# Keep-warm products, another order behind attention, and five instead of four of eight chunks turned by DMA, in a fused attention and mixture-of-experts kernel

## The chip, the core and the metric

The kernel runs on one core of a Trainium2 chip. The metric is the device time of one execution in microseconds (us), median of several runs. The core's engines are TensorE (PE; its weight loads are shown apart as PEld), VectorE (DVE), ScalarE (ACT) and GpSimd (POOL); SyncE (SP) issues all the kernel's DMAs. Each engine works through its own list of instructions in order, and they wait for one another through semaphores.

## The reference

Three stages follow one another, all in fp32.

```python
# 1. gated linear attention: 4 batches, 8 heads, 768 steps, head size 40; state C (40x40), n, m per head
m_new = max(f + m, i); f_s = exp(f + m - m_new); i_s = exp(i - m_new)
C = f_s * C + i_s * outer(v, k);  n = f_s * n + i_s * k
y = sigmoid(o_gate) * (C @ q) / max(abs(n . q), 1)          # x: 3072 tokens x 320
# 2. soft mixture: 8 experts x 4 slots
logits = x @ phi                                             # 3072 x 32
d = softmax(logits over tokens);  slot_input = d.T @ x       # 32 x 320
slot_out = relu(slot_input @ w1[e]) @ w2[e]                  # 320 -> 1024 -> 320 for each expert
x = softmax(logits over slots) @ slot_out
# 3. dense block
h = x @ w_in                                                 # 3072 x 1024
u = h * softmax(h);  ln = (u - mean(u)) / sqrt(var(u) + 1e-6) * g_ln
out = ln @ w_out                                             # 3072 x 320
```

## The kernel before, in words

**Attention.** The tokens are cut into 24 units of 128 tokens (6 chunks of the sequence times 4 batches). A unit's work is cut into some forty steps, and strings of step names (`FIRST`, `ORDER`, `LAST`, lines 33 to 50) give the order in which all engines' instructions are written, unit by unit; no scheduler changes it. In the last two units (`LAST`) the step `qm` (L524) multiplies the queries of unit 23 by decay factors on GpSimd, `x` (L360) forms a unit's gated output on GpSimd, `sl` (L439) adds a group of four units into the slot sums, and `mean` (L509) averages the output weights with the product of a constant and `wsum`, a sum of weight blocks that GpSimd forms (L741). A unit's output lies in one of five buffers `x_t`, used in turn. Next to all this the weights are loaded and decoded. Early on, `warm_up(6)` (L538) runs products whose result nobody reads.

**Behind attention.** Lines 747 to 949 are a chain for the last unit and the experts: its output is normalised, transposed (L763) and multiplied by `phi` for all four units of the group together (L772, `lt_last`), the maximum is taken (L775), weights of the softmax are formed, slot inputs summed and transposed (L804, `siT`), then come the experts' first and second products (L836, L893), the slots' outputs times `w_in` (L934, `swc_ps`) split into a high and a low fp32r part (`swh`, `swl`) and spread into two tiles `swf` (L947, L948). `w_low` (L927) makes the low part of the output weights on VectorE.

**The dense block.** 24 tiles of 128 tokens are pipelined. `FIN_START` (L56) orders the filling of the pipeline, `FIN` (L57) each later tile; a token such as `e:3` writes step `e` for the tile three ahead. The steps:

- `h` (L962): two products on TensorE give 1024 values a token; `m` (L967) their maximum, on VectorE; `e` (L974) exp, on ScalarE; `u` (L981) their product, on VectorE.
- `T0` (L1008): TensorE transposes four of the eight 128-column chunks of u into PSUM. The other four go through DMA: `d` (L1014) copies them on GpSimd into two planes of 16-bit halves (`up`), `t` (L1019) lets a DMA transpose these into `tp`, and `g` (L1024) joins the halves on GpSimd into `uf`. Tiles 0 and 1 use TensorE for all eight.
- `x0`, `x1` (L1031 on ScalarE, L1029 on GpSimd): the high fp32r part `uh` of each half; `y0`, `y1` (L1035, VectorE): the low part `ul`.
- `k0` to `k7`, `a`, `b` (L1043, L1044, L1046): three products for each chunk; `a` is the two with `uh`, `b` the one with `ul`.
- `q`, `s`, `v`: variance and scale; `o` (L1050): scaled output on ScalarE, and its DMA.

Of the kernel before, what the change touches and what calls it, by code (L numbers as in the profile page):

```python
# [7 lines left out]
F32 = mybir.dt.float32  # L8
# [4 lines left out]
U16 = mybir.dt.uint16  # L13
# [6 lines left out]
T = TOK = 128  # L20
# [19 lines left out]
 "numa xT tm1 scA numb scB den0 xTc tm2 nt ntc sig0 R o0 den2 o1 exp sg sig1 kw o3 wA wB o2 sl qm x sig2",  # L40
 "one o0 o1 o2 o3 xT numa numb xTc den0 den2 sg mean x",
# [14 lines left out]
FIN_START = "c:1 h:0 cc:1 m:0 c:2 h:1 c:3 cc:2 m:1 e0:0 e1:0 u0:0 c:4 e0:1 T0:0 x0:0 cc:3 u1:0 u0:1 T1:0 y0:0 cc:4 h:2 x1:0 m:2 c:5 y1:0 e1:1 v:0 T0:1 u1:1 e:2 x0:1 u:2 k0:0 a6:0 q:0 a4:0 d:2 a5:0 cc:5 b4:0 b6:0 s:0 y0:1 a7:0 k3:0 b5:0 k1:0 h:3 k2:0 m:3 b7:0 T1:1 T0:2 x1:1 v:1 y1:1 k0:1 e:3 a7:1 t:2 v:2 x0:2 u:3 a6:1 o:0 q:2 k3:1 h:4 k2:1 b4:1 b5:1 y0:2 a5:1 b6:1 g:2 k1:1 a4:1 d:3 m:4 q:1 h:5 e:4 k0:2 m:5 t:3 x1:2 b7:1 g:3 T0:3 k1:2 x0:3 a4:2 y1:2 k3:2 a5:2 a7:2 u:4 b4:2 d:4 s:1 o:1 a6:2 e:5 k2:2 y0:3 b6:2 s:2 v:3 b5:2 t:4 x1:3 b7:2"  # L56
# [7 lines left out]
def tile_kernel(  # L64
# [441 lines left out]
    def wo_mean(fs):  # L506
        wm = GT["warm"][:, 1].rearrange("p r t -> p (r t)")[:, 0:DM]
        for f in fs:
            PE.matmul(wm, on128, wo[:, 5 + f, :] if f else wsum, start=f == 0, stop=f == 2)  # L509
        return wm  # L510
# [84 lines left out]
    pe_gate(0)  # L595
    gate_nat(0)
# [24 lines left out]
    def ops(i):  # L621
# [31 lines left out]
        else:  # L653
            T["one"] = po_last
            T["mean"] = lambda: wo_mean(range(2))
        if i == NU - 2:
            T["R"], T["exp"], T["qm"] = pe_qscale, st_qscale, st_qmul
# [57 lines left out]
    for i in range(NU):  # L715
# [33 lines left out]
    ph0 = ps_sc.tile([128, 512], F32, tag="s1", name="ph0")  # L749
    A.activation(out=ph0, in_=ones[:, 0:1].to_broadcast([128, 512]), func=AF.Copy, scale=0.0)  # L750
    pe_xT(L - 1)
    st_xT(L - 1)
    U[L]["sg"] = kvo_t[L % 4][:, 2 * DM + NH:].rearrange("p (h d) -> p h d", h=NH)
# [13 lines left out]
    lg = bank("misc", "lt_last")  # L767
    PE.matmul(lg[:, 128:129], ident, lt_t[:, T:T + 1], start=True, stop=True)
    for k in range(3):
        kk = min(128, DM - 128 * k)  # L770
        for j in range(NB):
            PE.matmul(lg[32 * j:32 * j + 32, 0:128], phi_sb[0:kk, k, :], U[4 * g + j]["xT"][0:kk, k, :], start=k == 0, stop=k == 2)  # L772
    wm = wo_mean([2])
# [27 lines left out]
    A.copy(out=lt_t[:, 0:T], in_=lt)  # L801
    siT = [bank(t, f"siT{k}")[:, 0:NS] for k, t in enumerate(("pr", "dps", "po"))]
# [15 lines left out]
    ltT = bank("misc", "ltT")  # L818
    PE.transpose(ltT[:, 0:128], lt_t[:, 0:T], ident)
    tot = GT["warm"][:, 0, 1]  # L820
    A.copy(out=nat[:, NB * g:NU].rearrange("p j s -> p (j s)"), in_=ltT[:, 0:128])
    PE.matmul(tot[:, 0:1], sel, fst[:, 1:2], start=True, stop=True)
# [28 lines left out]
    w1_mm(0, range(5))  # L851
# [72 lines left out]
    def w_low(*qs):  # L924
        for q in qs:
            f = slice(q * FC // 4, (q + 1) * FC // 4)
            V.tensor_tensor(out=wl[:, f], in0=wo[:, f], in1=wh[:, f].bitcast(F32), op=ALU.subtract)  # L927

    w_low(0, 1)
# [8 lines left out]
    w_low(2)  # L938
# [3 lines left out]
    for n in range(2):  # L942
# [5 lines left out]
        cp[n](sw[n], sw_ps)  # L948
    w_low(3)
# [49 lines left out]

    def f_T(i, n):  # L1000
# [6 lines left out]
        for k in range(4):  # L1007
            PE.transpose(ps[:, k, :], F[i]["u"][:, (4 * n + k) * 128:(4 * n + k + 1) * 128], ident)  # L1008
        F[i]["uT", n] = ps

    def f_planes(i):
        if i in DT:
            F[i]["up"] = fx.tile([128, 2, 512], U16, tag="up", name=f"up{i}")
            G.tensor_copy(out=F[i]["up"], in_=F[i]["u"][:, 512:DF].bitcast(U16).rearrange("p (n two) -> p two n", two=2))  # L1014

    def f_turn(i):
        if i in DT:
            F[i]["tp"] = fx.tile([128, 2, 4, 128], U16, tag="tp", name=f"tp{i}")
# [14 lines left out]
    def f_lo(i, n):  # L1033
        c = slice(4 * n, 4 * n + 4)
# [119 lines left out]
```

## Time and profile before

| what | value |
|---|---|
| median of 3 runs (lowest, highest) | 284.1 us (283.4, 284.36) |
| profiled execution | 284.2 us, span 282.4 us from the first to the last instruction |
| PE busy | 267.7 us (95%), 3293 instructions |
| DVE, ACT, POOL busy | 243.1 us (86%), 216.9 us (77%), 149.6 us (53%) |
| granted TensorE clock | 1.000 of full speed over the span |
| attention | to about 135 us of the span |
| behind attention, filling the pipeline | about 135 to 197 us |
| dense block with a steady beat | about 197 to 270 us |
| last three tiles | to 282.4 us |

The span's times below count from its first instruction. In a row of the timeline stand start, duration, engine, line, operation, result from operands, and in brackets how long the engine was idle before it and what ended that.

### The profile page before, as it was taken

The numbers are of one execution on the slowest core, as the hardware profiler recorded it, in microseconds if no ns is written. First come the engines' busy times: TensorE is split into PE (matmuls) and PEld (weight loads), VectorE is DVE, ScalarE is ACT, GpSimd is POOL, SyncE is SP. The second block draws the span as 40 slices with busy tenths as digits, with TensorE's granted clock in tenths as the row PEclk, the third lists the DMA queues.
The fourth block names the chain that finished last, engine by engine and source line by source line (L and its number), as shares of the span: only waits on it lengthen the run. The fifth ranks groups of instructions, "written<-read, shape, count | busy, mean of one in ns | idle before, by whom it ended". The sixth has DMA issues, their size and how long they took to land.

```text
span 282.4 us, 8484 instructions
## 1 busy us (share of the span) xinstructions
PE 267.7 (95%) x3293; PEld 216.9 (77%) x3293; DVE 243.1 (86%) x514; ACT 216.9 (77%) x513; POOL 149.6 (53%) x179
## 2 busy tenths in 40 slices
PE   8899989999999999999899998999999999999995
PEld 5676767777777776867533367998999999999994
DVE  7999787998998997996579699999999999899950
ACT  6798957998789786797436758996877878778763
POOL 5754433654555555348106400556868767676760
PEclk9999999999999999999999999999999999999999
DMA  5898997999999998999999100246445364443531
GB/s 156 276 290 296 311 318 277 317 300 269 296 313 285 300 282 263 295 260 381 364 362 360 51 0 2 60 89 129 106 94 111 84 99 100 91 105 94 99 86 46
DMA packets 48808, 56.63 MB, mean 201 GB/s; under 512 B 26816, under 2 KB 38720, under 8 KB 48768
## 3 DMA queue, kind: packets, MB, share of 16 engines
q1 hardware_dynamic: 48768, 56.09, 67.6%
q8 instruction: 26, 0.43, 0.6%
q14 instruction: 14, 0.11, 0.1%
HBM read 46.38 MB, written 3.93 MB: 178 GB/s over the span
## 4 chain that ended last, share of the span: by engine, by line
PE 78%; DVE 6%; ACT 5%; issue 4%; DMA 4%; POOL 3%; POOLq 0%; ACTq 0%; SPq 0%; DVEq 0%
PE o L1046 9%; PE o L1043 9%; PE o L1044 9%; PE sc L280 8%; PE po L298 7%; PE R L244 4%; PE pr L301 4%; PE uT L1008 4%; PE h L962 3%; PE ph L836 3%; PE xTp L365 3%; PE so_ps L893 3%; DMA w2s<-w 3%; PE R L247 2%; PE dps L308 2%
## 5 line engine op out<-in xcount | busy, mean ns | idle before, releaser
L1043 PE MATMUL o<-wh,uh 128*128 128x320 f32 x192 | 60.3, 320 | 0.3 <-POOL uh L1029 0.3
L1044 PE MATMUL o<-wl,uh 128*128 128x320 f32 x192 | 58.2, 309 | 0.0
L1046 PE MATMUL o<-wh,ul 128*128 128x320 f32 x192 | 47.9, 310 | 0.1
L1014 POOL COPY up<-u 128x1024 uint16<-128x1024 uint16 x22 | 23.3, 1058 | 33.4 <-issue 16.1
L1024 POOL COPY uf<-tp 128x1024 uint16<-128x1024 uint16 x22 | 32.1, 1458 | 10.2 <-DMA tp<-up 10.1
L1043 PEld LDWEIGHTS o<-wh,uh 128*128 128x128 f32 x192 | 36.1, 188 | 1.5 <-POOL uh L1029 0.6
L1044 PEld LDWEIGHTS o<-wl,uh 128*128 128x128 f32 x192 | 36.1, 188 | 0.9
L1046 PEld LDWEIGHTS o<-wh,ul 128*128 128x128 f32 x192 | 33.0, 188 | 0.6 <-DVE ul L1035 0.6
L284 DVE TENSOR_TENSOR lb<-sc,lb 128x512 f32<-128x512 f32 x48 | 31.1, 674 | 1.9 <-PE sc L280 1.9
L967 DVE TENSOR_REDUCE st<-h 128x1 f32<-128x1024 f32 x24 | 29.2, 1220 | 0.3 <-PE h L962 0.2
L298 PE MATMUL po<-kvo,lb 128*64 128x41 f32 x544 | 27.2, 227 | 2.0 <-issue 2.0
L253 ACT ACTIVATE lb<-R 64x512 f32<-64x512 f32 (+1 forms) x48 | 25.5, 580 | 2.7 <-PE R L247 2.6
L1050 ACT ACTIVATE ob<-o,st 128x320 f32<-128x320 f32 x24 | 12.7, 529 | 18.9 <-ACT ga L974 8.4
L298 PEld LDWEIGHTS po<-kvo,lb 128*64 128x64 f32 x544 | 22.4, 137 | 5.1 <-issue 3.4
L280 PE MATMUL sc<-qk 64*128 64x128 f32 x288 | 23.1, 289 | 0.0
L280 PEld LDWEIGHTS sc<-qk 64*128 64x128 f32 x288 | 18.6, 187 | 4.2 <-issue 2.7
L1035 DVE TENSOR_TENSOR ul<-uf,uh 128x512 fp32r<-128x512 f32 x22 | 20.7, 941 | 1.2 <-POOL uh L1029 1.2
L981 DVE SCALAR_TENSOR_TENSOR u<-h,ga 128x1024 f32<-128x1024 f32 (+1 forms) x17 | 19.6, 1157 | 2.0 <-ACT ga L974 1.8
L1035 DVE TENSOR_TENSOR ul<-uT,uh 128x512 fp32r<-128x512 f32 x26 | 17.8, 684 | 2.8 <-ACT uh L1031 2.7
L261 ACT ACTIVATE kvo<-kvo 128x320 f32<-128x320 f32 x36 | 17.0, 472 | 3.8 <-DMA kvo<-kvo 1.9
L301 PE MATMUL pr<-C,qk 128*64 128x82 f32 x224 | 19.5, 249 | 0.0
L244 PE MATMUL R<-gr,gl 128*128 128x512 f32 x48 | 17.3, 442 | 1.1 <-ACT lb L253 1.1
(285 smaller groups left out, 708.9 us busy)
## 6 DMA issues: line engine op xcount, KB each, us to landing
w1s<-w1p SPq DMA_DIRECT2D x19, 512.0 KB
w2s<-w SPq DMA_DIRECT2D x7, 1280.0 KB
kvo<-kvo SPq DMA_DIRECT2D x15, 484.0 KB
out<-ob SPq DMA_DIRECT2D x24, 160.0 KB
qk<-qkp SPq DMA_DIRECT2D x18, 160.0 KB
qk<-qkp SPq DMA_DIRECT2D x36, 80.0 KB
kvl<-kvo SPq DMA_DIRECT2D x5, 484.0 KB
raw<-w SPq DMA_DIRECT2D x4, 512.0 KB
```

Source lines behind the costliest of these rows:

```text
L244: PE.matmul(U[u]["R"][:, a], gl_t[c % 2][:, b, :], gr_t[c % 2][:, a * NR:(a + 1) * NR, :], start=True, stop=False)
L253: A.activation(out=lb[p, :, :, t], in_=U[u]["R"][p, :, :, t], func=AF.Exp)
L280: PE.matmul(U[u]["sc", a][:, r, :], t[p, 0, r, :], t[p, 1, r, :], start=True, stop=True)
L284: V.tensor_tensor(out=lb[:, a * NR:(a + 1) * NR, :], in0=U[u]["sc", a], in1=lb[:, a * NR:(a + 1) * NR, :], op=ALU.mult)
L298: PE.matmul(U[u]["po"][t, 2 * r + a, 0:DV], U[u]["lb"][:, a * NR + r, t], va(u, 2 * r + a), start=not last or r + a == 0, stop=not last)
L301: PE.matmul(U[u]["po" if last else "pr"][t, 2 * r:2 * r + 2, 0:DV], qk_t[u % 4][:, 1, r, t], C_t[b][:, r, :].rearrange("p (a d) -> p a d", ...
L967: V.tensor_reduce(out=F[i]["st"][:, 0:1], in_=F[i]["h"], axis=AX.XY, op=ALU.max, negate=True)
L1024: G.tensor_copy(out=uf.rearrange("p k t -> p (k t)").bitcast(U16).rearrange("p (n two) -> p n two", two=2), in_=F[i]["tp"].rearrange("p tw ...
L1035: V.tensor_tensor(out=F[i]["ul"][:, c, :], in0=F[i]["uT", n], in1=F[i]["uh"][:, c, :].bitcast(F32), op=ALU.subtract)
L1043: PE.matmul(o, uh, wh[:, k, :], start=k == 0, stop=False)
L1044: PE.matmul(o, uh, wl[:, k, :], start=False, stop=False)
L1046: PE.matmul(o, ul, wh[:, k, :], start=False, stop=k == FC - 1)
```

## The change

What it does, part by part:

1. Products that nobody reads: two fp32 products of 320 columns in the first unit, after the first `pe_gate` (`warm1`), and step `w:0`, three such products ahead of the first tile's transposes.
2. The last two units: unit 21's output goes to a free part of `win` (`x_of`) instead of one of the five buffers, and its step `x` stands ahead of `sig1`; `qm` runs on VectorE; `wsum` is summed earlier; `mean` is cut into three calls at other places.
3. Behind attention: the logits of unit 20, of 21 and 22, and of 23 are three groups of products instead of one; unit 22's transposes use another bank; the transpose `ltT` and product `tot` stand after the first group of the experts' products; `w_low` is ordered otherwise; `swf` is copied in four pieces instead of two.
4. The dense block: from tile 4 on (`DT5`) three chunks are transposed on TensorE and five by DMA; of these tiles the even ones have their DMA half's high part on GpSimd as before, the odd ones on ScalarE; `x1` stands after `e`, `k3` is cut into `a3` and `b3`.
5. The last tile's scaled output is made half on ScalarE, half on VectorE.

```diff
- "numa xT tm1 scA numb scB den0 xTc tm2 nt ntc sig0 R o0 den2 o1 exp sg sig1 kw o3 wA wB o2 sl qm x sig2",
- "one o0 o1 o2 o3 xT numa numb xTc den0 den2 sg mean x",
+ "numa xT tm1 scA numb scB den0 xTc tm2 nt ntc sig0 R o0 den2 o1 exp sg x sig1 kw o3 wA wB o2 sl qm sig2",
+ "one o0 o1 o2 o3 xT numa numb xTc den0 den2 sg x",
-FIN = "o:-1 u:2 d:2 t:2 h:3 m:3 q:0 k0:0 T0:1 T1:1 k1:0 x0:1 g:1 x1:1 y1:0 y0:1 k2:0 k3:0 s:0 a4:0 a5:0 e:3 a6:0 a7:0 v:1 b4:0 b5:0 b6:0 b7:0"
+FIN = "o:-1 u:2 d:2 t:2 h:3 m:3 q:0 k0:0 T0:1 T1:1 k1:0 x0:1 g:1 y1:0 y0:1 k2:0 a3:0 s:0 a4:0 a5:0 e:3 x1:1 a6:0 a7:0 v:1 b3:0 b4:0 b5:0 b6:0 b7:0"
+DT5 = range(4, 24)
+    def x_of(u):
+        return win[:, 3, 0:384] if u == NU - 3 else x_t[u % NX]
-        G.tensor_tensor(out=q, in0=q, in1=dsc_t.bitcast(F32), op=ALU.mult)
+        V.tensor_tensor(out=q, in0=q, in1=dsc_t.bitcast(F32), op=ALU.mult)
     pe_gate(0)
+    warm_up(2, ps_o.tile([128, 512], F32, tag="pr", name="warm1"))
...
+    wo_mean([1])
+    pe_xT(L - 1, "pr")
     st_xT(L - 1)
+    last_logits((0,))
...
+    last_logits((1, 2))
+    last_logits((3,))
+    wo_mean([2])
...
+    wm = wo_mean([0])
     siT = [bank(t, f"siT{k}")[:, 0:NS] for k, t in enumerate(("pr", "dps", "po"))]
-    w1_mm(0, range(5))
+    w1_mm(0, range(1))
+    ltT = bank("misc", "ltT")
...
+    PE.matmul(tot[:, 0:1], sel, fst[:, 1:2], start=True, stop=True)
+    w1_mm(0, range(1, 5))
...
-        cp[n](sw[n], sw_ps)
+            cp[1 - j](sw[n][:, 256 * j:256 * j + 256], sw_ps[:, 256 * j:256 * j + 256])
...
+    def split_at(i):
+        return 3 if i in DT5 else FC // 2
-        if n and i in DT:
+        if n and i in DT and (i % 2 == 0 or i not in DT5):
             G.tensor_copy(out=out, in_=in_)
         else:
             A.copy(out=out, in_=in_)
...
+        n = DM // 2 if i == NU - 1 else DM
+        A.activation(out=ob[:, 0:n], in_=F[i]["o"][:, 0:n], func=AF.Copy, scale=F[i]["st"][:, 7:8])
+        if n < DM:
+            V.tensor_scalar(out=ob[:, n:], in0=F[i]["o"][:, n:DM], scalar1=F[i]["st"][:, 7:8], scalar2=None, op0=ALU.mult)
+    F_OP["w"] = lambda n: [PE.matmul(F[0]["uT"].rearrange("p k t -> p (k t)")[:, 0:DM], ident, wo[:, f, :], start=True, stop=True) for f in range(3)]
```

## Rows read from the trace of the kernel before

**Rows 1.** Page, part 2: granted TensorE clock in 40 slices, tenths.
```profile
PEclk9999999999999999999999999999999999999999
```
**Rows 2.** Stretch of steady tiles: us, busy of PE, PEld, DVE, ACT, POOL; clock, DMA.
```profile
196.66:262.96 66.30, 66.30 (x453) 64.91 (x452) 62.87 (x122) 54.33 (x120) 49.11 (x47) 1.00 0.48 99
```
**Rows 3.** Chain that ended last, steady tiles: start, us, engine, tile, line.
```profile
254.28 0.46 PE h L962 x2
255.18 0.44 PE uT L1008 x4
258.70 0.46 PE h L962 x2
```
**Rows 4.** Timeline of POOL and DVE, steady tiles: copies that meet.
```profile
242.65 1.72 POOL L1024 COPY uf<-tp 128x1024 uint16<-128x1024 uint16 x1
247.07 1.16 POOL L1024 COPY uf<-tp 128x1024 uint16<-128x1024 uint16 x1
...
242.66 0.68 DVE L1035 TENSOR_TENSOR ul<-uf,uh 128x512 fp32r<-128x512 f32 x1
247.08 1.70 DVE L1035 TENSOR_TENSOR ul<-uf,uh 128x512 fp32r<-128x512 f32 x1
```
**Rows 5.** Timeline of POOL and DVE, tiles 4 to 6.
```profile
194.32 1.04 POOL L1014 COPY up<-u 128x1024 uint16<-128x1024 uint16 x1
195.45 1.48 POOL L1024 COPY uf<-tp 128x1024 uint16<-128x1024 uint16 x1
...
194.41 1.50 DVE L1035 TENSOR_TENSOR ul<-uf,uh 128x512 fp32r<-128x512 f32 x1 [0.59 <-POOL uh L1029]
```
**Rows 6.** Timeline of ACT, DVE, POOL: one steady turn of the tiles.
```profile
263.21 0.53 ACT L1050 ACTIVATE ob<-o,st 128x320 f32<-128x320 f32 x1 [0.76 <-ACT ga L974]
264.77 0.57 ACT L1031 CAST uh<-uT 128x512 fp32r<-128x512 f32 x1
...
266.89 1.23 DVE L981 SCALAR_TENSOR_TENSOR u<-h,ga 128x1024 f32<-128x1024 f32 x1 [0.46 <-ACT ga L974]
...
266.54 0.61 POOL L1029 CAST uh<-uf 128x512 fp32r<-128x512 f32 x1
268.19 1.44 POOL L1014 COPY up<-u 128x1024 uint16<-128x1024 uint16 x1 [1.04 <-ACT ob L1050]
```
**Rows 7.** Timeline of POOL and PE: tiles 2 and 4 come out of the DMA.
```profile
181.03 1.16 POOL L1024 COPY uf<-tp 128x1024 uint16<-128x1024 uint16 x1 [3.22 <-DMA tp<-up]
...
187.44 1.04 POOL L1014 COPY up<-u 128x1024 uint16<-128x1024 uint16 x1
192.53 1.17 POOL L1024 COPY uf<-tp 128x1024 uint16<-128x1024 uint16 x1 [2.50 <-DMA tp<-up]
...
194.43 0.41 PE L1043 MATMUL o<-wh,uh 128*128 128x320 f32 x1 [0.29 <-POOL uh L1029]
```
**Rows 8.** Timeline of DVE, POOL and PE: end of attention.
```profile
132.70 0.50 DVE L327 TENSOR_TENSOR num<-pr,nat 128x328 f32<-128x328 f32 x1 [2.56 <-POOL x L360]
...
130.62 1.28 POOL L524 TENSOR_TENSOR qk<-qk,dsc 128x512 f32<-128x512 f32 x1 [1.01 <-ACT dsc L520]
...
134.47 0.81 PE L509 MATMUL warm<-cd,bsc 128*128 128x320 f32 x2 [0.55 <-POOL cd L741]
135.12 0.70 PE L509 MATMUL warm<-wo,bsc 128*128 128x320 f32 x2
137.20 1.00 PE L772 MATMUL lt_last<-xT,phi_sb 128*32 128x128 f32 x24
140.77 0.65 PE L804 MATMUL siT<-cst,acc 128*128 128x32 f32 x4 [0.30 <-ACT lt L801]
```
**Rows 9.** Timeline of PE: where keep-warm products are added.
```profile
10.52 0.73 PE L244 MATMUL R<-gr,gl 128*128 128x512 f32 x2 [0.72 <-ACT lb L253]
...
170.60 1.27 PE L1008 MATMUL uT<-cst,u 128*128 128x128 f32 x8 [1.75 <-DVE u L981]
```
**Rows 10.** Timeline of ACT: the last tile's output.
```profile
279.06 0.53 ACT L1050 ACTIVATE ob<-o,st 128x320 f32<-128x320 f32 x1 [1.30 <-PE o L1046]
```

More of the change, by code (lines that the diff above doesn't have):

```diff
@@ L508, in wo_mean @@
         for f in fs:
-            PE.matmul(wm, on128, wo[:, 5 + f, :] if f else wsum, start=f == 0, stop=f == 2)
+            PE.matmul(wm, on128, wo[:, 5 + f, :] if f else wsum, start=f == 1, stop=f == 0)
         return wm
@@ L654, in ops @@
             T["one"] = po_last
[L655 removed]
         if i == NU - 2:
+            G.memset(x_of(NU - 3)[:, DM + 1:384], 0.0)
+            G.memset(x_of(NU - 3)[:, DM:DM + 1], 1.0)
             T["R"], T["exp"], T["qm"] = pe_qscale, st_qscale, st_qmul
@@ L748, in tile_kernel, with last_logits @@
     cp = (lambda out, in_: V.tensor_copy(out=out, in_=in_), lambda out, in_: A.copy(out=out, in_=in_))
-    ph0 = ps_sc.tile([128, 512], F32, tag="s1", name="ph0")
-    A.activation(out=ph0, in_=ones[:, 0:1].to_broadcast([128, 512]), func=AF.Copy, scale=0.0)
-    pe_xT(L - 1)
+    wo_mean([1])
+    pe_xT(L - 1, "pr")
     st_xT(L - 1)
+    lg = bank("misc", "lt_last")
+    PE.matmul(lg[:, 128:129], ident, lt_t[:, T:T + 1], start=True, stop=True)
+    def last_logits(js):
+        for k in range(3):
+            kk = min(128, DM - 128 * k)
+            for j in js:
+                PE.matmul(lg[32 * j:32 * j + 32, 0:128], phi_sb[0:kk, k, :], U[4 * g + j]["xT"][0:kk, k, :], start=k == 0, stop=k == 2)
+    last_logits((0,))
     U[L]["sg"] = kvo_t[L % 4][:, 2 * DM + NH:].rearrange("p (h d) -> p h d", h=NH)
@@ L766, in tile_kernel @@
         cp[k % 2](xT[:, k, :], xp[k])
[L767 to L773, printed above, removed]
+    ph0 = ps_sc.tile([128, 512], F32, tag="s1", name="ph0")
+    A.activation(out=ph0, in_=ones[:, 0:1].to_broadcast([128, 512]), func=AF.Copy, scale=0.0)
+    last_logits((1, 2))
+    last_logits((3,))
+    wo_mean([2])
     st, lt = gst_t[g % 2], lg[:, 0:128]
@@ L817, in tile_kernel @@
         )
[L818 to L822, printed above, removed]
     so_ps = ps_sc.tile([128, 512], F32, tag="s0", name="so_ps")
@@ L849, in hidden_ev @@
             )
-    w1_mm(0, range(5))
+    w1_mm(0, range(1))
+    ltT = bank("misc", "ltT")
+    PE.transpose(ltT[:, 0:128], lt_t[:, 0:T], ident)
+    tot = GT["warm"][:, 0, 1]
+    A.copy(out=nat[:, NB * g:NU].rearrange("p j s -> p (j s)"), in_=ltT[:, 0:128])
+    PE.matmul(tot[:, 0:1], sel, fst[:, 1:2], start=True, stop=True)
+    w1_mm(0, range(1, 5))
     V.tensor_scalar(out=fst[:, 2:3], in0=tot[:, 0:1], scalar1=1e-9, scalar2=None, op0=ALU.add)
@@ L917, in tile_kernel, with w_low @@
         PE.matmul(soT_ps[2][64 * k:64 * k + 64], so[:, 256:DM], ident, start=True, stop=True)
+    def w_low(*qs):
+        for q in qs:
+            f = slice(q * FC // 4, (q + 1) * FC // 4)
+            V.tensor_tensor(out=wl[:, f], in0=wo[:, f], in1=wh[:, f].bitcast(F32), op=ALU.subtract)
+    w_low(0)
     for k in range(3):
@@ L922, in tile_kernel @@
         )
[L924 to L929, printed above, removed]
+    w_low(1, 2)
     swc_ps = bank("misc", "swc_ps")[:, 0:256]
@@ L998, in f_scale, with ks @@
         A.activation(out=st[:, 7:8], in_=st[:, 6:7], func=AF.Exp, scale=-0.5)
+    def split_at(i):
+        return 3 if i in DT5 else FC // 2
+    def ks(i, n):
+        c = split_at(i)
+        return slice(c * n, c + (FC - c) * n)
     def f_T(i, n):
@@ L1072, in tile_kernel @@
             done.add((op, int(i)))
+            done.update((p + op[1], int(i)) for p in "ab" if op[0] == "k")
     for i in range(NU + 1):
```

51 lines of the change are left out of this document (25 added, 26 removed).

## The prediction

> **What bounds the kernel now.** I read first the granted clock [rows 1], then the table by stretches [rows 2], the chain of waits for the steady tiles [rows 3], and the timelines of the engines beside them. TensorE's clock is full in every slice: no stretch before is slowed by it. From 196.66 to 262.96 us TensorE is busy for all 66.30 us, VectorE for 62.87 of them [rows 2]. One tile takes 258.70 - 254.28 = 4.42 us of TensorE [rows 3]; VectorE has some 5% left. So whatever comes off TensorE there counts once, until another engine's ring is longer than the new beat. Elsewhere the kernel is a chain through all engines: at the end of attention VectorE stands idle for 2.56 us because GpSimd is late [rows 8], while the pipeline fills TensorE waits for tile 4 [rows 7].
>
> All sums are made against the profiled execution, 284.2 us (span 282.4 and 1.8 around it). The median of the runs shown is 284.1, so 0.1 comes off at the end.
>
> **Keep-warm products.** A pair of instructions (one fp32 product of 320 columns) takes 135.12 - 134.47 = 0.65 us [rows 8]. `warm1` is two, 1.3 us. The gap ahead of the second unit's decay product is 0.72 us, from 9.80 to 10.52 [rows 9], so they end near 11.0: between nothing (if they start earlier than the modelled end of the product before) and 0.6 late. ScalarE's exp and the unit behind wait for that product, and I see no spare time on ScalarE soon after; loads of later units, which wait for buffers, may take some of it in. +0.25, range 0 to 0.6. `w:0` is three, 1.95 us, in a gap of 1.75 [rows 9]: +0.2, range 0 to 0.3. What they could return is a clock that would fall without them; [rows 1] has none that falls, so 0.
>
> The Trainium skill ("TensorE: Matmul & The Clock Gate", Part 1) says that the clock halves when the engine has been too little busy, which is the reason one would add such products. The trace does not bear it out for these gaps: no slice is under 9 tenths. By the page they might be worth something, by the rows they are cost.
>
> **The last two units.** VectorE's step at 132.70 waits for GpSimd's `x` of unit 21, which stands behind `qm`, 130.62 and 1.28 long [rows 8]. Now `x` goes first, into a place that is free, and `qm` is on VectorE at about 0.7 (an estimate from the 0.68 of a two-operand 512-column step [rows 4]); it still needs the exp that released it at 130.6. So the step starts near 131.3, 1.4 sooner, or 1.0 if `qm` meets GpSimd's `x` as the two engines meet in [rows 4]. The wait of 0.55 for `wsum` at 134.47 goes too, but was covered by the same chain. TensorE then has unit 20's logits (between a quarter of the 1.00 that the whole group takes and all of it [rows 8]; I take 0.65) ahead of unit 23's transposes, which takes back 0.5 to 0.65; of the logits themselves only unit 23's 0.65 is left on the path. So the maximum comes 0.5 to 0.9 sooner. Then `wo_mean([0])`, 0.65, is put into a gap of 0.30 ahead of `siT` [rows 8] and takes 0.35 back. Moving `ltT` and `tot` behind the first expert products changes the order and not the amount: cover for them is the same busy TensorE. Taken: -0.45, range -0.9 to +0.1. The pieces of `swf` and the earlier `w_low` let the first `h` start 0.3 sooner, since two half copies go on two engines: -0.3, range -0.4 to 0.
>
> **Tile 4.** It is the first with five chunks, and already late: its copy starts at 187.44, its planes land for the join at 192.53, and TensorE waits 0.29 for the high part [rows 7]. With 640 instead of 512 columns the copy takes 0.24 more (1.04 x 0.25, less the fixed part), the DMA by the same scaling up to 0.35, the join 0.26, the cast 0.14; TensorE needs it one chunk earlier (0.3), and the low part then meets tile 6's copy. All on one path: about 1.0 to 1.4 if nothing ahead of it has become later still, 0.2 if the DMA's wait was an accident of its neighbours (192.53 - 188.48 = 4.05 from the copy's end, where tile 2 took 3.22 [rows 7]). I take +0.7.
>
> **Steady tiles.** Four transposes take 0.44 [rows 3], 0.11 each; 20 tiles save one: -2.2 if TensorE stays the bound, at a beat of 4.31. Is it? VectorE's low parts have as many columns as before (384 + 640 instead of 512 + 512). ScalarE: its own steps are paced by TensorE with an idle 0.76 a tile [rows 6]; by the 0.57 of 512 columns [rows 6] `x0` gets some 0.11 shorter, and an odd tile's `x1` adds some 0.58, which fits there. But `x1` waits for the join, and `o`, `q` and all that follows on ScalarE are queued behind it. GpSimd: copy, join and cast (1.04 + 1.16 + 0.61 [rows 4 to 6]) grow by 0.64 on even tiles and shrink on odd ones.
>
> This makes a ring over two tiles, and it decides. From the start of an even tile's copy: copy 1.28; then VectorE's low part, which waits for the copy's end (as at 194.41 [rows 5]), holds GpSimd for 0.68; join done 1.29 after that, so 3.25 in all; cast on ScalarE 0.63 with its signal; then ScalarE's next output to exp and to u, 266.89 - 263.21 = 3.68 less the 0.11 of `x0` [rows 6]; u and signal to the next copy 268.19 - 266.89 = 1.30 [rows 6]. Sum 8.75 for two tiles, against 8.62 for TensorE. The ring is longer by 0.13, a scaled number that may be off by as much. Its lateness first eats 0.8 us of slack: `b3` starts some 3.6 after a tile's `h`, counting 0.147 a product ((4.42 - 0.46 - 0.44) / 24 [rows 3]), the low part ends at 2.8; if tile 4 has used that up, the tiles from 6 to 20 gain only (8.84 - 8.75) / 2 = 0.045 each, 0.7, plus 0.2 for tiles 4 and 5 and 0.3 for the last three: -1.2. I take -1.7, between the two.
>
> **The last output** is one ScalarE step of 0.53 [rows 10]; half of it beside half on VectorE saves about 0.1.
>
> Sum: +0.25 + 0.2 - 0.45 - 0.3 + 0.7 - 1.7 - 0.1 = -1.4: 282.8 profiled, 282.7 as a median.
>
> **The rivals.**
>
> *TensorE stays the bound throughout* (the ring is under 8.62, tile 4 costs 0.2): +0.25 + 0.2 - 0.75 + 0.2 - 2.2 - 0.1 = -2.4: 281.7. For it: ScalarE and VectorE both have idle time in [rows 6]. Against it: the join waits for everything in turn.
>
> *It all cancels*: keep-warm +0.6, the end of attention gives -0.4, tile 4 costs 1.3, the ring binds at -1.2, the end -0.1: 0.2 more, 284.3 profiled, 284.2. Here the change doesn't do what it says: transposes leave TensorE, and TensorE waits in their place. For it: tile 4's wait is in [rows 7] already.
>
> *Slower, by the meeting of join and low part.* At 242.65 and 242.66 join and low part start as one, and the low part has its 0.68; at 247.07 and 247.08 the join goes first and the low part takes 1.70 [rows 4]: a toss. With the longer copy the low part waits already when the copy ends, and at 194.41 it then went ahead of the join [rows 5]; that is one case. Should the join go first, the low part ends 1.42 - 0.06 = 1.36 later, and with the ring bound TensorE waits for that at `b3` for 0.6 to 1.3. Two such tiles eat the gain, three make the change slower; with four of the 15 it is +3.6 on the forecast, 286.3. The Trainium skill ("SBUF — State Buffer", Who interferes with whom) calls it an exclusive lock that whoever starts first holds for its whole instruction; it does not say who gets it when both wait, so it speaks for longer holds with five chunks and leaves the toss open. By it alone the time would be that of this rival or of the forecast.
>
> **How the numbers follow.** About 0.3% (0.85 us) is what a measurement of this kernel can tell from no change: faster is below 283.25, slower above 284.95. Forecast 0.40 (own range 282.1 to 283.5, of it 0.36 faster), TensorE-bound 0.20, all faster; cancelled 0.24, of it 0.22 the same; lock 0.16, slower. With 0.04 of the forecast the same and 0.02 of the cancelled slower: faster 0.56, same 0.26, slower 0.18. The range goes from 280.9 (the second case with its gains at their bounds) to 285.6, which leaves out the worse half of the lock case.
>
> **What would show it.** In the profile after: the beat of TensorE from `h` to `h` in the steady tiles: 4.31 if TensorE binds, 4.38 if the ring does; the wait of `b3` for the low part; join and low part durations (0.8 or over 2); tile 4's wait on TensorE, 1 us or more; VectorE's wait of 2.56 gone; the second unit's decay product at 11.0; the granted clock still full. The forecast is wrong if the beat is over 4.42, if tile 4 waits less than before, or if the part before 142 us got longer.

## The result: slower by 1.2%

The changed kernel takes 289.14 us (median of 6 runs, 287.45 to 294.19) against 284.87 us (6 runs) before: ratio 1.0123, interval 1.0076 to 1.0169. The forecast of 282.7 us, faster, was wrong. The profiled execution took 287.45 us with a span of 285.6 us. (Ratios leave disturbed runs out and medians don't, so for some kernels below the two differ.)

How long attention takes differs by 4.8 us between two executions of one and the same kernel (experiment `e7_before`), so I compare distances between landmarks behind it: the end of the last scores product (A), the maximum of the last logits (B), the end of the second layer's products `so_ps` (C), the first `h` (D), `h` of tile 8 (E), `h` of tile 23 (F), and the end. Differences of starts and ends in the timelines, in us (the end is that of the span, which is printed to 0.1 us):

| | A-B | B-C | C-D | D-E | E-F | F-end | A-end |
|---|---|---|---|---|---|---|---|
| before | 10.09 | 22.74 | 5.26 | 30.37 | 66.30 | 19.44 | 154.20 |
| after | 9.87 | 24.11 | 6.49 | 30.93 | 65.44 | 20.35 | 157.19 |
| after - before | -0.22 | +1.37 | +1.23 | +0.56 | -0.86 | +0.91 | +2.99 |

Only the first and the fifth column gained. 2.99 us is 1.06% of the span, most of the ratio.

**A-B.** Timeline of VectorE and TensorE after, end of attention. In brackets: idle before, and what ended it.
```profile
130.77 0.69 DVE L528 TENSOR_TENSOR qk<-qk,dsc 128x512 f32<-128x512 f32 x1 [0.46 <-ACT dsc L524]
131.39 0.53 DVE L328 TENSOR_TENSOR num<-pr,nat 128x328 f32<-128x328 f32 x1
134.18 0.53 DVE L773 TENSOR_TENSOR xx<-xx,rd 128x320 f32<-128x320 f32 x1
...
135.01 0.96 PE L765 MATMUL lt_last<-xT,phi_sb 128*32 128x128 f32 x6
135.90 0.55 PE L778 MATMUL xT_last<-cst,xx 128*128 128x128 f32 x3
136.38 1.86 PE L765 MATMUL lt_last<-xT,phi_sb 128*32 128x128 f32 x18
...
138.28 0.29 DVE L788 TENSOR_REDUCE gst<-lt_last 128x1 f32<-128x129 f32 x1 [0.87 <-PE lt_last L765]
```
The wait of 2.56 us [rows 8] is gone and `num` starts 2.98 us behind A instead of 4.50. But unit 20's 6 products alone take 0.96, as long as all 24 took in one lot [rows 8], and unit 23's transposes stand behind them: its result is there at 134.71 and is turned 1.19 us later, at 135.90. So the maximum starts only 0.22 us sooner behind A.

**B-C.** A stretch before, then three stretches after (columns as in [rows 2]), then, after, what the DMA-issuing queue SP waited for between 136 and 165 us, and TensorE's timeline.
```profile
140.00:142.00 2.00, 1.70 (x31) 1.25 (x23) 1.10 (x5) 0.96 (x6) 0.28 (x1) 1.00 1.07 363
...
138.00:140.00 2.00, 2.00 (x28) 1.19 (x30) 0.57 (x2) 0.94 (x4) 0.22 (x1) 1.00 1.07 358
140.00:142.00 2.00, 2.00 (x30) 1.29 (x22) 1.12 (x5) 0.85 (x5) 0.28 (x1) 1.00 0.47 161
142.00:144.00 2.00, 2.00 (x23) 0.65 (x19) 0.69 (x4) 0.43 (x2) 0.00 (x0) 1.00 0.71 147
```
```profile
SPq L497 <- PE warm L513: 7.4, 1, 7.4
```
```profile
140.39 0.81 PE L513 MATMUL warm<-cd,bsc 128*128 128x320 f32 x2
153.02 4.49 PE L908 MATMUL so_ps<-w2s,h 128*8 128x320 f32 x62
157.92 4.47 PE L908 MATMUL so_ps<-w2s,h 128*8 128x320 f32 x58 [0.41 <-DMA w2s<-w]
```
A load of the second layer's weights stood for 7.4 us until `wo_mean([0])` at 140.39 had read `wsum`, which lies in the memory that the load fills. The DMA fell from 358 to 161 and 147 GB/s for 4 us, where before it stayed at 363, and at the other end TensorE ran short of weights: its 120 products run slower and stop for 0.41 (9.37 us from first to last, 8.26 before).

**C-D.** Timeline after of TensorE, ScalarE and VectorE around `swf`:
```profile
166.13 0.38 PE L963 MATMUL sw_ps<-swl,scratch 128*128 128x256 f32 x1
166.55 0.37 ACT L754 CAST swf<-sw_ps 128x256 fp32r<-128x256 f32 x1 [0.16 <-PE sw_ps L963]
166.98 0.38 PE L963 MATMUL sw_ps<-scratch 128*128 128x256 f32 x1 [0.46 <-ACT swf L754]
168.18 0.39 PE L963 MATMUL sw_ps<-scratch 128*128 128x256 f32 x1 [0.46 <-ACT swf L754]
168.79 0.42 DVE L754 CAST swf<-sw_ps 128x256 fp32r<-128x256 f32 x1 [0.78 <-PE sw_ps L963]
168.88 0.89 PE L977 MATMUL h<-swf,cT 128*128 128x512 f32 x2
```
Both halves of `swf` lie in one bank. The second half's product waits until the first is copied out, which leaves TensorE idle twice for 0.46 us, and the pipeline of product and copy became a chain.

**D-E, tile 4.** Timeline after of GpSimd, VectorE, TensorE:
```profile
190.13 1.26 POOL L1037 COPY up<-u 128x1280 uint16<-128x1280 uint16 x1
194.86 1.40 POOL L1047 COPY uf<-tp 128x1280 uint16<-128x1280 uint16 x1 [1.71 <-DMA tp<-up]
196.32 0.72 POOL L1052 CAST uh<-uf 128x640 fp32r<-128x640 f32 x1
...
197.08 1.84 DVE L1058 TENSOR_TENSOR ul<-uf,uh 128x640 fp32r<-128x640 f32 x1 [0.28 <-POOL uh L1052]
...
197.10 0.42 PE L1066 MATMUL o<-wh,uh 128*128 128x320 f32 x1 [0.40 <-POOL uh L1052]
```
TensorE's wait for the high part is 0.40 (0.29 [rows 7]), and the low part takes 1.84, beside the copy of tile 6, which started ahead of it (196.99). That it is not worse hangs on the turn by the DMA: tile 4's was joined 3.44 us after its issue, before 4.02. Where it took 4.16 with five chunks (`e1_swf`), TensorE waited longer:
```profile
203.41 0.42 PE L1066 MATMUL o<-wh,uh 128*128 128x320 f32 x1 [1.11 <-POOL uh L1052]
```
At landings that are alike, late in e1 and before or early after and in `e4_four` (3.12), the way from `h` of tile 6 to that of tile 8 is 11.17 against 9.98 and 10.42 against 9.08 us: the fifth chunk costs 1.2 to 1.3 us there. Why the turn lands sooner or later stays open.

**E-F.** Stretch of 15 tiles after, then `h`, the GpSimd copies of two even tiles, and `u`, over one turn of two tiles:
```profile
199.81:265.25 65.44, 65.44 (x438) 63.16 (x436) 60.37 (x120) 58.02 (x127) 52.85 (x38) 1.00 0.53 115
```
```profile
230.34 0.62 PE L977 MATMUL h<-swf,cT 128*128 128x512 f32 x2
234.75 0.62 PE L977 MATMUL h<-swf,cT 128*128 128x512 f32 x2
239.06 0.62 PE L977 MATMUL h<-swf,cT 128*128 128x512 f32 x2
...
231.94 1.25 POOL L1037 COPY up<-u 128x1280 uint16<-128x1280 uint16 x1 [0.78 <-DVE u L996]
240.67 1.25 POOL L1037 COPY up<-u 128x1280 uint16<-128x1280 uint16 x1 [0.23 <-DVE u L996]
...
230.64 1.23 DVE L996 SCALAR_TENSOR_TENSOR u<-h,ga 128x1024 f32<-128x1024 f32 x1 [0.59 <-ACT ga L989]
239.37 1.22 DVE L996 SCALAR_TENSOR_TENSOR u<-h,ga 128x1024 f32<-128x1024 f32 x1 [0.59 <-ACT ga L989]
```
The beat alternates between 4.41 and 4.31 us, 4.363 on average over the 15 tiles (65.44 / 15), against 4.42. From `u` to `u` over two tiles and from copy to copy it is 8.73 us: the ring of the prediction (8.75), not TensorE (8.62). Its parts agree too: from the copy at 231.94 to the cast on ScalarE (235.16), the output (235.80), `u` (239.37) and the next copy (240.67) it takes 3.22, 0.64, 3.57 and 1.30 us, for 3.25, 0.63, 3.57 and 1.30. TensorE counts as busy throughout, so its busy share does not show this wait; the beat does.

**F-end.** Timeline after of the last tile:
```profile
272.12 1.34 SPq L1042 DMA_TRANSPOSE tp<-up  x1
...
277.25 1.40 POOL L1047 COPY uf<-tp 128x1280 uint16<-128x1280 uint16 x1 [2.43 <-DMA tp<-up]
...
282.01 0.39 ACT L1074 ACTIVATE ob<-o,st 128x160 f32<-128x160 f32 x1 [0.48 <-PE o L1069]
...
282.44 0.39 DVE L1076 TENSOR_SCALAR ob<-o,st 128x160 f32<-128x160 f32 x1 [2.17 <-ACT ob L1074]
```
No later tile covers the turn by the DMA here: five chunks are joined 5.1 us after their issue, join, cast and low part are each longer, and TensorE waits 0.46 us for them (279.46). It hangs on the landing: in `e8_cold`, with the same dense block, the last turn was joined 3.8 us after its issue, TensorE did not wait, and F-end is 19.68. The join there:
```profile
277.47 1.40 POOL L1046 COPY uf<-tp 128x1280 uint16<-128x1280 uint16 x1 [1.09 <-DMA tp<-up]
```
With four chunks there was room: the last turn was joined 4.6 to 4.8 us after its issue in e5, e6 and e12, and F-end stayed at 19.35 to 19.39. The two halves of the last output go one after the other, 0.82 us where the whole took 0.53 [rows 10].

### The profile page after: what moved, and what is told of

Its sections match the earlier page's. It is cut to its first block, busy times and chain, and to the rows that moved or that the text cites. A ratio compares the mean times of both kernels' runs of the same rounds, so it can differ in the third digit from the quotient of the medians.

```text
span 285.6 us, 8466 instructions
## 1 busy us (share of the span) xinstructions
PE 271.7 (95%) x3283; PEld 217.0 (76%) x3283; DVE 243.6 (85%) x517; ACT 221.9 (78%) x524; POOL 154.6 (54%) x170
## 4 chain that ended last, share of the span: by engine, by line
PE 65%; DMA 17%; DVE 7%; POOL 4%; issue 3%; ACT 2%; POOLq 1%; SPq 1%; ACTq 0%; DVEq 0%
PE o L1069 8%; PE o L1066 8%; PE o L1067 8%; PE sc L281 6%; DMA qk<-qkp 5%; PE po L299 5%; DMA win<-qkp 4%; PE h L977 3%; PE R L245 3%; PE pr L302 3%; DMA w2s<-w 3%; PE xTp L369 3%; PE uT L1031 3%; PE warm L542 2%; DMA kvl<-kvo 2%
## 5 line engine op out<-in xcount | busy, mean ns | idle before, releaser
L1047 POOL COPY uf<-tp 128x1280 uint16<-128x1280 uint16 (+1 forms) x22 | 40.2, 1825 | 11.4 <-DMA tp<-up 11.4
L1069 PE MATMUL o<-wh,ul 128*128 128x320 f32 x192 | 45.5, 315 | 0.3 <-DVE ul L1058 0.2
L1037 POOL COPY up<-u 128x1280 uint16<-128x1280 uint16 (+1 forms) x22 | 27.1, 1234 | 30.6 <-issue 18.0
L1069 PEld LDWEIGHTS o<-wh,ul 128*128 128x128 f32 x192 | 31.9, 188 | 1.9 <-DVE ul L1058 0.8
L299 PE MATMUL po<-kvo,lb 128*64 128x41 f32 x544 | 26.6, 227 | 1.3 <-issue 1.1
L1058 DVE TENSOR_TENSOR ul<-uf,uh 128x640 fp32r<-128x640 f32 (+1 forms) x22 | 22.9, 1039 | 4.3 <-ACT uh L1054 2.5
L299 PEld LDWEIGHTS po<-kvo,lb 128*64 128x64 f32 x544 | 21.7, 137 | 4.2 <-issue 2.3
L1008 ACT ACTIVATE ga<-u,st 128x1024 f32<-128x1024 f32 x16 | 18.3, 1144 | 0.0
L989 ACT ACTIVATE ga<-h,st 128x1024 f32<-128x1024 f32 (+1 forms) x17 | 18.0, 1062 | 0.1
```

Source lines behind the costliest of these rows:

```text
L299: PE.matmul(U[u]["po"][t, 2 * r + a, 0:DV], U[u]["lb"][:, a * NR + r, t], va(u, 2 * r + a), start=not last or r + a == 0, stop=not last)
L1037: G.tensor_copy(out=F[i]["up"], in_=F[i]["u"][:, 128 * split_at(i):DF].bitcast(U16).rearrange("p (n two) -> p two n", two=2))
L1069: PE.matmul(o, ul, wh[:, k, :], start=False, stop=k == FC - 1)
```

## The experiments

All distances and, where timed, the ratio to the kernel before (5 rounds):

| | A-B | B-C | C-D | D-E | E-F | F-end | A-end | ratio |
|---|---|---|---|---|---|---|---|---|
| e1_swf | 10.42 | 24.00 | 5.25 | 31.56 | 65.44 | 20.22 | 156.89 | 1.007 (1.002 to 1.0121) |
| e2_mean | 10.21 | 22.88 | 6.51 | 30.94 | 65.45 | 20.40 | 156.39 | 1.0075 (1.003 to 1.012) |
| e3_mean_ltt | 10.19 | 22.77 | 6.50 | 30.95 | 65.45 | 20.51 | 156.37 | 1.0088 (1.0041 to 1.0134) |
| e4_four | 9.85 | 23.94 | 6.49 | 29.58 | 66.30 | 19.77 | 155.93 | 1.0055 (1.0004 to 1.0106) |
| e5_repaired | 10.21 | 22.77 | 5.26 | 30.50 | 64.84 | 19.39 | 152.97 | 0.9994 (0.995 to 1.0039) |
| e6_xt_first | 9.35 | 22.77 | 5.27 | 30.53 | 64.86 | 19.35 | 152.13 | 0.995 (0.9911 to 0.9988) |
| e7_before | 10.09 | 22.75 | 5.26 | 30.40 | 66.30 | 19.53 | 154.33 | |
| e8_cold | 9.86 | 23.85 | 6.89 | 31.33 | 65.45 | 19.68 | 157.06 | |
| e9_four_xt | 9.36 | 22.86 | 5.24 | 30.36 | 66.30 | 19.50 | 153.62 | 1.0062 (1.0017 to 1.0108) |
| e10_cold_xt | 9.35 | 22.76 | 5.27 | 31.15 | 64.82 | 19.36 | 152.71 | 0.995 (0.9906 to 0.9994) |
| e11_dense | 10.08 | 22.73 | 5.28 | 30.56 | 64.85 | 19.30 | 152.80 | 0.9955 (0.9888 to 1.0021) |
| e12_banks | 9.36 | 22.93 | 5.07 | 29.68 | 64.84 | 19.35 | 151.23 | 0.9914 (0.9875 to 0.9954) |

Untouched columns repeat within 0.2 us in most profiles, so one profile tells apart what the ratios, each uncertain by 0.4 to 0.7%, can't. The exceptions are D-E and F-end, which follow the landing of one turn by the DMA, A-B in e1, and the stretches in which the clock fell (e8, e10).

**e7_before: the kernel before, a second profile.**

> The kernel before once more, for a second profile. Theory (how long attention takes, and how long h of tile 7 to h of tile 8 takes, hangs on how soon the DMA lands in that execution, not on the code): the maximum of the logits falls anywhere from 138 to 142 us, 5.35 us from h of tile 7 to that of tile 8 is not seen again but about 4.4; the beat of 4.42 us, 28.0 us from the maximum to the first h, and 19.4 us from the last h to the end are. Rival (they belong to the code): all as in the first profile within 0.2 us.

Attention ended at 132.97 us instead of 128.20. Waits of this execution up to there, for a unit's `kvo` (us in total, times, longest):
```profile
ACT kvo L261 <- DMA kvo<-kvo: 6.3, 5, 2.6
POOL kvo L269 <- DMA kvo<-kvo: 6.1, 4, 3.8
```
Together 12.4 us, where the first profile has 1.9 and 5.0. So that attention hangs on the loads held (the maximum fell at 143.06, past the 138 to 142 expected), and the rest was wrong: 5.35 us from `h` of tile 7 to that of tile 8 came again. From A on the two executions differ by 0.13 us.

**e1_swf and e12_banks: the copies of `swf`.** In e1, on the changed kernel; in e12, on e6:
```diff
-            cp[1 - j](sw[n][:, 256 * j:256 * j + 256], sw_ps[:, 256 * j:256 * j + 256])
+        cp[n](sw[n], sw_ps)
```
```diff
-        sw_ps = bank(("po", "pr")[n], f"sw_ps{n}")
         for j in range(2):
+            sw_ps = bank(("po", "pr", "dps", "misc")[2 * n + j], f"sw_ps{n}_{j}")
...
+            cp[1 - j](sw[n][:, 256 * j:256 * j + 256], sw_ps[:, 256 * j:256 * j + 256])
-        cp[n](sw[n], sw_ps)
```


> The changed kernel with swf copied in two whole copies again, one on VectorE and one on ScalarE, instead of four pieces; all else stays. Theory A (the pieces lock TensorE and ScalarE step by step: the next product into the same bank waits for the copy of the first half): the time from the end of swl to the first product of h falls from 2.81 us to about 1.55, as before, and the whole time falls by 1.2 us, to about 1.008 of the kernel before. Rival (the stretch is long because the delayed weights of the second expert push other ScalarE work into it): the stretch stays near 2.8 us and the ratio stays at 1.012.

> As e6_xt_first, with swf copied in four pieces again, each piece's products in a bank of PSUM of its own instead of two pieces to a bank. Theory (the pieces were dear because the second piece's products wait until the first piece of the same bank is copied out, not because small copies are slow): no wait for a copy between the products, and from the end of swl to the first h 1.2 to 1.4 us, 0.2 to 0.3 less than with whole copies (1.55) and far less than with two pieces to a bank (2.81); ratio 0.994. Rival (ScalarE's small copies are the cost): 2 us or more.

From the end of `swl` to the first `h`: 2.81 us in the changed kernel, 1.56 in e1, 1.38 in e12. (Two other stretches of e1's profile are longer, both at a granted clock of 1.00: A-B by an idle 0.41 of TensorE that the profile puts down to no wait, D-E by the late turn of tile 4.) e12's timeline of TensorE, ScalarE and VectorE, the same place as above:
```profile
164.91 0.39 PE L960 MATMUL sw_ps<-swl,scratch 128*128 128x256 f32 x1
165.13 0.28 PE L960 MATMUL sw_ps<-scratch 128*128 128x256 f32 x1
165.25 0.28 PE L960 MATMUL sw_ps<-swl,scratch 128*128 128x256 f32 x1
...
165.33 0.85 ACT L754 CAST swf<-sw_ps 128x256 fp32r<-128x256 f32 x2 [0.17 <-PE sw_ps L960]
165.57 0.90 DVE L754 CAST swf<-sw_ps 128x256 fp32r<-128x256 f32 x2
...
166.23 0.80 PE L974 MATMUL h<-swf,cT 128*128 128x512 f32 x2
```
No product waits for a copy. So the pieces are right and their place was wrong: the sharing of a bank costs 1.43 us (2.81 - 1.38), small copies nothing. (e12 gives each piece a bank and a PSUM tile of its own; which of the two the program's wait is for, no run tells apart.) The Trainium skill ("PSUM — Partial Sum Buffer", Terms) calls it an error if TensorE writes a bank while another engine reads it; no run here shows the error; in this trace the one always waited for the other. The two engines write the two halves of each `swf` at the same time here, from two banks. So a shared output tile does not by itself force turns; the halves of the last output, which do go in turn, also read one bank. With 282.40 us (median of 12 runs; before 285.99) e12 has the lowest ratio of this study; its interval overlaps that of e6, and from B to D both take 28.0 us. Of its A-end of 151.23 us some 0.8 is chance: in that execution the turn of tile 4 landed early and D-E is 29.68.

**e2_mean and e3_mean_ltt: who holds the weights' memory.** In e2 the product of `wsum` moves forward; e3 also takes `ltT` and `tot` back ahead of `w1_mm(0, range(5))`.
```diff
-            PE.matmul(wm, on128, wo[:, 5 + f, :] if f else wsum, start=f == 1, stop=f == 0)
+            PE.matmul(wm, on128, wo[:, 5 + f, :] if f else wsum, start=f == 1, stop=f == 2)
...
-    wo_mean([1])
+    wo_mean([1, 0])
     pe_xT(L - 1, "pr")
...
-    wo_mean([2])
+    wm = wo_mean([2])
...
-    wm = wo_mean([0])
```


> The changed kernel with the product of wsum issued right behind the first product of the mean (ahead of xT of the last unit but one) instead of behind the slot sums of the last unit; all else stays. Theory B (this product is the last reader of memory that a weight load of the second layer wants, so the load's queue stands still until 141.0 us): the hole of the DMA engines at 140 to 144 us goes or shrinks to under 1 us, the second expert's products end 1 to 1.3 us sooner, and the time falls by 1 to 1.3 us, ratio about 1.008. Rival (the transpose ltT, moved behind the first group of the hidden layer, holds the next load in the same way, or the products wait for VectorE's chain that became 1.1 us later): the hole moves to ltT's end at about 142.8 us, the gain is under 0.4 us.

> As the kernel with the product of wsum moved forward, and ltT, its copy and the total moved back ahead of all products of the hidden layer. Theory B: no more than the wsum move alone gives, within 0.3 us. Rival (ltT holds the second load): most of the 1.3 us comes only here; the end of the second expert's products goes back to 161.1 us and the softmax over the rows to 147.9 us, ratio about 1.0075.

e2's stretch behind the place of the hole, SP's wait for the same reader, and the products (its attention ended 1.7 us later than in the first profile after):
```profile
142.00:144.00 2.00, 1.70 (x28) 1.03 (x23) 1.12 (x5) 0.93 (x6) 0.28 (x1) 1.00 1.07 362
```
```profile
SPq L497 <- PE warm L513: 1.2, 1, 1.2
```
```profile
154.94 8.26 PE L907 MATMUL so_ps<-w2s,h 128*8 128x320 f32 x120
```
The hole is gone (362 GB/s here, 364 in the 2 us ahead of it), the wait fell from 7.4 to 1.2 us, the 120 products run in one piece, and B-C is 1.23 us shorter. e3 adds 0.11: `ltT` hardly matters. Both pay 0.3 in A-B, where the moved product stands ahead of the last logits.

**e6_xt_first: the order of the last logits.** On e5 (below); the turn of unit 23 is issued first, then units 0, 1, 2 of the group in one lot.
```diff
-    last_logits((0,))
...
-    last_logits((1, 2))
+    last_logits((0, 1, 2))
     last_logits((3,))
```


> As e5_repaired, but TensorE turns the last unit's result before any product of the logits, and the products of units 0, 1 and 2 of the group go in one lot while the turned result is copied out. Theory (the 1.3 us that VectorE gained at the end of attention were eaten because the first unit's products stand in TensorE's order ahead of the turn): the maximum of the logits follows the last scores 0.7 to 1.0 us sooner than in e5_repaired, and h starts as much sooner. Rival (the second layer's products wait for their weights from the DMA, whenever the hidden layer is done): the maximum comes sooner, and the time from it to h grows by the same 0.7 to 1.0 us.

A-B is 9.35 us against 10.21 in e5 and 10.09 before, and nothing is given back: B-C and C-D stay. So the weights didn't bind, and the gain on VectorE had been lost to TensorE's order.

**e4_four, e5_repaired, e9_four_xt, e11_dense: the fifth chunk.** e4 is the changed kernel with `DT5 = range(0)`. e5 has e3's and e1's edits and the two below; e9 is e6 with `DT5 = range(0)`; e11 is the kernel before with only e5's dense block.
```diff
-DT5 = range(4, 24)
+DT5 = range(6, 22)
...
-        n = DM // 2 if i == NU - 1 else DM
+        n = DM
```


> The changed kernel with four chunks of u turned by the DMA in every tile, as before (the range of tiles with five is empty); the parts ahead of the dense block stay changed. Theory C (the five chunks give 0.75 us over 14 tiles and take 0.5 us at tile 4 and 0.9 us at the last tile): the time falls by about 0.6 us, ratio 1.010; the beat is 4.42 us a tile, up from 4.37, and the last h is 19.4 us ahead of the end instead of 20.35. Rival (the ring bound of the five chunks is worth its full gain, and all loss lies ahead of the dense block): the time rises by 0.7 us, ratio 1.015.

> The changed kernel with four things put back and one narrowed: wsum's product early, ltT ahead of the hidden layer, swf in two whole copies, the last output in one piece, and five chunks by the DMA in tiles 6 to 21 only. Theory: from the last maximum of the logits to the first product of h it takes 28.0 us as before (30.6 in the changed kernel); from h of tile 0 to h of tile 8 it takes 30.4 us or less, the beat in the tiles with five chunks is 4.37 us, and from the last h to the end it takes 19.45 us as before. Sum against before 0.7 us less, ratio 0.9975, with a bound of 1.000. Rival (five chunks cost wherever they are let in, 1 us at the first such tile and something at the last): no part gained, ratio 1.000 to 1.003.

> As e6_xt_first, with four chunks by the DMA in every tile. Theory (five chunks, kept away from the first and the last tiles, give 0.09 us or more a tile): from the first h to the end 1.2 to 1.5 us longer than in e6_xt_first (114.7 us), so 115.9 to 116.2 as in the kernel before; ratio 0.998. Rival (the dense block's order of products, not the fifth chunk, brings it, as e4_four's 115.65 us hints): under 115.7 us, and 4.4 us instead of 5.35 from h of tile 7 to h of tile 8.

> The kernel before with nothing but the dense block of e5_repaired: five chunks by the DMA in tiles 6 to 21. Theory (this is the only part of the change that gains by itself): from the first h to the end 114.7 us against 116.1 before, the stretch ahead of it unchanged, ratio 0.995. Rival (the lead that lets TensorE run at 4.30 us a tile in e5_repaired comes from the keep-warm products ahead of the first tile): the beat alternates 4.30 and 4.43, gain 0.7 us or less.

With four chunks E-F is 66.30, with five from tile 4 on 65.44, with five from tile 6 on 64.84 to 64.86. e5's turn:
```profile
227.02 0.62 PE L975 MATMUL h<-swf,cT 128*128 128x512 f32 x2
235.63 0.63 PE L975 MATMUL h<-swf,cT 128*128 128x512 f32 x2
...
227.06 1.23 DVE L994 SCALAR_TENSOR_TENSOR u<-h,ga 128x1024 f32<-128x1024 f32 x1 [0.59 <-ACT ga L987]
235.81 1.22 DVE L994 SCALAR_TENSOR_TENSOR u<-h,ga 128x1024 f32<-128x1024 f32 x1 [0.59 <-ACT ga L987]
```
VectorE's ring is the same (8.75 us), but TensorE goes at 4.305 a tile (half of 235.63 - 227.02), where 4.37 was expected of e5: `u` starts 0.04 after `h` at the one end and 0.18 after it at the other, so the ring falls behind by 0.14 a turn, and there is room for that until near the end. In the changed kernel `u` starts 0.30 after `h` in every turn. Tile 4 had used the room up, as far as the runs tell: only which tiles get five chunks makes the difference, for e1, e2 and e3, which undo other parts, keep the 65.44. From D to the end e5 takes 114.73 us and e11 114.71, the kernel before 116.11, e9 116.16, the changed kernel 116.72: the fifth chunk is worth 1.4 us by itself where it stays away from the first and last tiles. (e11's ratio alone, from few runs, does not exclude 1.) As it was put in it gains nothing: of the 0.61 lost from D to the end, 0.27 is the halved output and 0.13 a later second half of `swf`, and some 0.2 is left for the fifth chunk. At the end, five chunks cost 0.58 (20.35 - 19.77, e4) where their turn lands late, and the halved output 0.27 (19.77 - 19.50, e9). e4's 29.58 in D-E misled me: there the turn of tile 4 landed 0.9 us sooner than in `e7_before`, and in e9, with the same dense block, D-E is 30.36.

e9's ratio is a miss: by A-end it should be faster than before, and it was slower. By its one profile the excess lies ahead of A (133.08 us), and there the granted clock was low for a while (0.57 from 44 to 52 us); but e9's executions at full clock are no faster than the kernel before either, and why stays open.

**e8_cold and e10_cold_xt: without keep-warm products**, on the changed kernel and on e6. `w:0` is left out of `FIN_START`, and
```diff
-    warm_up(2, ps_o.tile([128, 512], F32, tag="pr", name="warm1"))
```


> The changed kernel without either set of keep-warm products. Theory (TensorE had its full clock at both places in the kernel before, so they buy nothing and cost a few tenths at most): granted clock 1.0 in both stretches, h of tile 0 to h of tile 2 takes 5.3 to 5.45 us with and without them, the first decay products start 0.1 to 0.2 us sooner. Rival (the stretch runs at the lower clock without them): the granted clock falls under 0.9 there and the products of the stretch take longer.

> As e6_xt_first, without the two sets of keep-warm products. Theory (with swf in whole copies TensorE's gap ahead of h is short enough that the clock stays up): from the last scores to the end as in e6_xt_first, 152.1 us, within 0.3; granted clock 1.0 from the first h on, where e8_cold showed doubled durations. Rival (the products hold the clock up): the first products of h take about 1.1 us for two instead of 0.75, and the stretch is 0.4 us longer or more.

Stretches of TensorE alone (us, busy, granted clock, DMA share, GB/s), first of e6, then of e10, each from the place of `w:0` on:
```profile
173.00:175.00 2.00, 2.00 (x18) 1.00 0.03 8
```
```profile
170.00:172.00 2.00, 0.42 (x4) 1.00 0.00 0
172.00:174.00 2.00, 1.82 (x9) 0.73 0.00 0
174.00:176.00 2.00, 2.00 (x10) 0.50 0.00 0
```
Without `w:0` the clock fell to 0.50 (1.2 of 2.4 GHz) behind the gap, and D to `h` of tile 7 took 26.12 instead of 25.03 us. In e8 it fell just ahead of the first `h` (2 products 1.20 us instead of 0.89), behind the chain of `swf` copies and ahead of where `w:0` stands, so the lack of `w:0` did not cause that fall. In both profiles of the kernel before, and in that of e11, it didn't fall. So my theory is wrong. How often the products help can be counted: the mean granted clock was under 0.9965 (a line drawn for the count only) in 3 of 12 executions of e6 and in 7 of 12 of e10, and over all experiments in 28 of 97 executions with the products and in 69 of 131 without, more often without them on each of the four chips used. Falls during attention are included and the kernels differ in other ways too; what the products save in time is not shown, for the ratios of e6 and e10 are the same.

## Why the prediction was wrong

The step that failed is the part from A to D: the last two units and `swf` were put at -0.75 together, and that part is 2.38 us longer, for two waits that the prediction left out. From D to the end -0.9 was forecast (tile 4, steady tiles, last output and `w:0`), and +0.61 came, by terms that were mis-sized.

- *The last two units, -0.45.* Failed. The waits of VectorE and of `siT` were followed, but not who else waits for what was moved. "Changes the order and not the amount" holds for TensorE; the product of `wsum` is also the last reader of memory that a weight load wants (+1.23 of the 1.37 in B-C, e2). A-B gave 0.22 where 0.5 to 0.9 was forecast: unit 20's logits were to take back 0.5 to 0.65; they take 0.96 and stand ahead of the turn (e6), which now starts 1.19 us behind its result, before 0.08.
- *The pieces of `swf`, -0.3.* Failed: +1.23. Two half copies on two engines were counted, the bank that they share was not. With a bank for each the stretch is 0.18 shorter than with whole copies (1.38 against 1.56, e12 and e1), within the range of that term.
- *Tile 4, +0.7, range 0.2 to 1.4.* The number came out, in part by luck: D-E is +0.56, of it 0.13 from a later second half of `swf` (e4's 25.15 from D to `h` of tile 7, against 25.02), so about 0.43. The forecast's long case (1.0 to 1.4) is what five chunks cost at like landings, 1.2 to 1.3; the turn landed 0.6 us sooner than before. The TensorE wait of 1 us appeared in e1 only (1.11).
- *Steady tiles, -1.7.* The ring was right, 8.73 us measured for 8.75. Mis-sized was the slack: I went between -1.2 and -2.2; with the slack gone from tile 8 on, E-F gave 0.86. The last three tiles, which were to gain 0.3, cost 0.58, since no later tile covers the turn by the DMA there and it landed 5.1 us after its issue. e5 shows the other branch: with the slack left, TensorE's own 4.305.
- *The last output, -0.1.* Failed: +0.27. The halves went in turn. They read one bank and write one tile; by e12 the tile alone is not the reason, so the bank is the likely one, but no run gave the halves a bank each.
- *Keep-warm, +0.25 and +0.2.* `warm1` ran from 9.33 to 10.67, the second decay product came 0.15 us later behind the exp that frees it (10.27 against 10.07, before 10.52 against 10.47), and the next exp 0.35 later (2.59 us behind the first instead of 2.24), within the range; what is left of it at A no run shows; `w:0` fitted its gap (D-E is 30.50 in e5, with it, and 30.56 in e11, without). That the products return nothing held for the profile of before, and not for e10. The Trainium skill ("TensorE: Matmul & The Clock Gate", Part 1) has the clock halve when the engine has been too little busy. That was put aside because no slice showed it; e10 shows it, at 0.50 behind a stretch in which TensorE was busy for 0.42 of 2.00 us.
- *The rivals.* Join ahead of the low part, which was to make it slower, did not come about in the steady tiles: low parts take 0.94 there. VectorE and GpSimd met badly with a copy instead of a join, at tile 4 (1.84) and once behind F (1.91, where a low part alone takes 0.83). The change is slower for three reasons that no case had: the weights' memory, the bank, and the last tile. (The case in which it all cancels adds up to 284.4 profiled and 284.3 as a median, not 284.3 and 284.2.)

Of some 3.5 us (0.0123 x 284.87) the profiles show 3.0 behind A. The rest would lie ahead of A, where one kernel's executions differ by more; no run shows it.

## What to carry to other kernels

Before a reader is moved later, ask who waits for the memory it reads: a load's queue stalls without any engine showing it, and the bill comes 17 us on, as a wait for data. Splitting a copy out of PSUM in two pays here only where each piece has a bank of its own. And an edit that relieves the bound engine in steady state should leave out the first and the last turns, where what it lengthens has no cover. A single profile can flatter or blame such an edit by 0.9 us, by when one DMA lands; compare executions in which it landed alike.

## What the runs showed of the hardware

- A turn by the DMA (128 x 1024, 16 bit) was joined 3.1 us after its issue at tile 3, where the next came 5 us behind it, in both profiles of before. At tile 4, where the next came 2 us behind it, it took 4.0 us in seven profiles and 3.1 in two (e4, e12), so the next issue alone does not decide it. The last one, of 128 x 1280, took 5.0 to 5.2 us in four profiles and 3.8 in e8.
- Six products for 32 output partitions take as long as 24 in four sets of partitions, 0.96 against 1.00 us: the sets run beside one another.
- The same gap of 1.75 us left the clock at full in three profiles (both of before, e11) and let it fall to 0.50 in a fourth (e10).
- VectorE and ScalarE wrote two halves of one tile at the same time when they read them from two banks (e12).
